# Splitting the parts of w1 on ScalarE and VectorE, a plain F32 transform in the filter, and a first GEMM that ends tile by tile

## The chip, the core and the metric

The kernel runs on one core of one Trainium2 chip. The engines of a core work side by side, each through its own instructions in order: TensorE (PE, matrix products; PEld are its weight loads), VectorE (DVE), ScalarE (ACT), GpSimd (POOL) and SyncE (SP, which here only issues transfers). Transfers (DMA) are issued by SP or by POOL. The metric is the device time of one execution in microseconds; of several runs the median counts. The profile is of one execution and gives its span, from the first to the last instruction. TensorE's granted clock is given as a share of its full clock.

## The reference

Two branches read the same normalised input of 2048 tokens and 512 channels; the output is their product added to the input.

```python
def _A_ref(x, w_r, w_i):
    X = jnp.fft.rfft2(x, axes=(-2, -1))
    X = X * (w_r + 1j * w_i)
    return jnp.fft.irfft2(X, s=(S, D), axes=(-2, -1))

def _B_ref(x, w1, b1, w2, b2):
    h = _layernorm(x, axis=-1)
    u = _gelu(jnp.einsum("bsd,sf->bdf", h, w1) + b1)
    y = jnp.einsum("bdf,fs->bds", u, w2) + b2
    return y.transpose(0, 2, 1)

xn = _layernorm(x, axis=-1)
return x + _A_ref(xn, A_w_r, A_w_i) * _silu(_B_ref(xn, B_w1, B_b1, B_w2, B_b2))
```

S is 2048, D is 512 and the hidden size F is 1792. All of it is float32.

## The kernel before

The tokens lie as 16 blocks `j` of 128 partitions with 512 channels each, the hidden size is cut into 14 tiles of 128. The products of the two GEMMs are made in F32R, a reduced form of float32: each operand is split into a high part (a ScalarE copy into F32R) and a low part (the rest), and `mm3` (L116 to L119) adds three products, high x high, high x low and low x high. The helper `split` (L113) makes both parts, the high one on ScalarE and the low one on VectorE.

There are three stages.

1. **First half of the first GEMM** (loop of L349). For each block `j` the layer norm, the split of the normalised block into `hh[j]` and `hl[j]`, the split of w1's tiles 0 to 3 and 7 to 9, their products into seven of the eight PSUM banks (L316), and the first step of the Fourier transform along the sequence (`first_transform`, L191), folded by VectorE and GpSimd into `ey`.
2. **The filter, and the rest of the first GEMM beside it** (L403 to L562). `filter_steps` (L420) works off 16 groups of frequencies: a transform along the channels (L430, from `ey` and the constant `cd`), its result `sh`/`sl`, the transform along the sequence with the constant `gf` (`mm3`, L439), the multiplication with the filter on VectorE (L450 to L467, with ScalarE copies `zi` and `pq`), and the way back along the sequence (L490). Beside it `hidden_rest` (L523) makes the other seven tiles of the first GEMM in two batches: in the first all blocks `j` for tiles 4, 5, 10 and 11 (banks 7, 2, 0, 1), in the second all `j` for tiles 6, 12 and 13 (banks 7, 0, 1). One block of one batch is a *part*; 32 parts are loaded and split by `w1_part` (L497), three ahead of their use. Tiles 0 to 3 and 7 to 9 go through gelu (L248) at the start of this stage, tiles 4, 5, 10 and 11 between the batches, the rest behind the stage.
3. **The second GEMM** (loop of L693). It goes by a scheme of seven products in place of eight over blocks of 2 x 2: `forms` (L260) makes from the gelu results the tiles `fd`, `fa`, `fb`, `fc` (high and low, sums and differences), `w2_forms` (L593) makes the seven combinations of w2's quarters `a12`, `s1`, `a11`, `s4`, `a21`, each again high and low (L585, L586). One product is 21 instructions of 128x256 (L710), seven tiles times three. The way back of the spectral branch along the channels (L645, constant `ci`) and along the tokens (`spectral`, L668), the silu and the final product with the store run beside it.

`w1_part` is the piece that the change is about most. A raw part comes by SP into one of three buffers `w1s`; ScalarE writes the high part, writes its negative into the place of the low part, and GpSimd issues a transfer that adds the raw part to it:

```python
            A.activation(wq[:, 0], w, AF.Copy)
            A.activation(wq[:, 1], wq[:, 0].bitcast(F32), AF.Copy, scale=-1.0)
            G.dma_start(wq[:, 1], w, accum_op=ALU.add)
```

The order of the work in stage 2 is made by the loop of L549: in 19 steps the filter's generators are moved on with lags of 0, 1 and 3, 48 slots in all, and after each slot `rest` is moved on until 100 of the 112 tile products have been spread evenly over the slots; the last 12 (`LATE`) come behind, block by block (L622). The tile framework's scheduler then orders each engine's instructions. Buffers come from pools: a tile of a new pool in the place of an old one waits until the old tiles there are done with. The pools `us` (gelu results) and `w1q` (parts) take the place of `w1`, which closes at L404; `cd` is loaded at L411, behind that point.

Of the kernel before, what the change touches and what calls it, by code (L numbers as in the profile page):

```python
# [12 lines left out]
ALU = mybir.AluOpType  # L13
# [10 lines left out]
WARM = 16  # L24
LATE = 12
# [17 lines left out]
def _constants():  # L43
# [30 lines left out]
    for lo in range(16):  # L74
# [25 lines left out]
        "c_g": _parts(g, 2),  # L100
# [5 lines left out]
def spectral_mixer_kernel(tc, x, w1, b1, w2, b2, wk, we, wx, c_f, c_ft, c_d, c_i, c_g, c_h, out):  # L106
# [14 lines left out]
    with tc.tile_pool(name="ps", bufs=1, space=PSUM) as psp, ExitStack() as left, ExitStack() as right:  # L121
# [3 lines left out]
        cft = pers.tile([P, 2, P], F32R, name="cft")  # L125
        b1t = pers.tile([P, NF], F32, name="b1t")
# [14 lines left out]
        w1p = pool(lstage, "left", "w1", 3)  # L141
# [74 lines left out]
        def w1_load(j, f0, nf, up, wide):  # L216
            raw = up.tile([P, wide * P], F32, name=f"w1r{f0}_{j}", tag="w1r")
            SY.dma_start(raw[:, :nf * P], w1[:, j, f0 * P:(f0 + nf) * P])
            return raw[:, :nf * P]
# [4 lines left out]
        def hidden(j, banks, w):  # L224
            for i, bank in enumerate(banks):
                sl = slice(i * P, (i + 1) * P)
                mm3(ps[:, bank], w[0][:, sl], w[1][:, sl], hh[j], hl[j], j == 0, j == NJ - 1)
                yield
# [120 lines left out]
        for j in range(NJ):  # L349
# [54 lines left out]
        lstage.close()  # L404
# [3 lines left out]
        usp = pool(lstage, "left", "us", 3)  # L408
        w1q = pool(lstage, "left", "w1q", 3)
        cd = mp.tile([P, 4, P], F32, name="cd", bufs=1)  # L410
        SY.dma_start(cd, c_d)  # L411
# [8 lines left out]
        def filter_steps(n, lo):  # L420
            gf = mp.tile([P, 2, P], F32R, name=f"gf{lo}", tag="gf", bufs=3)
            G.dma_start(gf, c_g[lo])
# [8 lines left out]
            sh = mp.tile([P, D], F32R, name=f"sh{lo}", tag="sh")  # L431
            sl = mp.tile([P, D], F32R, name=f"sl{lo}", tag="sl")
            split(sh, sl, pd)
# [5 lines left out]
            mm3(px, gf[:, 0], gf[:, 1], sh, sl, True, True)  # L439
# [57 lines left out]
        def w1_part(j, runs):  # L497

            n = sum(r[1] for r in runs) * P
            w = w1q.tile([P, 4 * P], F32, name=f"w1s{runs[0][0]}_{j}", tag="w1s")[:, :n]  # L500
            f = 0
            for f0, nf in runs:
                SY.dma_start(w[:, f:f + nf * P], w1[:, j, f0 * P:(f0 + nf) * P])
                f += nf * P
            wq = w1q.tile([P, 2, 4 * P], F32R, name=f"w1q{runs[0][0]}_{j}", tag="w1q", bufs=4)[:, :, :n]
            A.activation(wq[:, 0], w, AF.Copy)  # L506
            A.activation(wq[:, 1], wq[:, 0].bitcast(F32), AF.Copy, scale=-1.0)  # L507
            G.dma_start(wq[:, 1], w, accum_op=ALU.add)  # L508
            return wq[:, 0], wq[:, 1]
# [13 lines left out]
        def hidden_rest():  # L523
            parts_ = [(j, *b) for b in BATCHES for j in range(NJ)]
            w = [w1_part(p[0], p[1]) for p in parts_[:3]]
            for i, (j, runs, banks) in enumerate(parts_):
                yield from hidden(j, banks, w.pop(0))
                if i + 3 < len(parts_):
                    w.append(w1_part(*parts_[i + 3][:2]))
                if i >= NJ:  # L530
                    passed[0] = j + 1
                if i == NJ - 1:
                    while waiting:
                        form_step()
                    for ft, bank in ((10, 0), (11, 1), (4, 7)):
                        gelu(ft, bank)
                    todo.extend([forms(3), forms(4)])
                    waiting.append([(5, 2)])

# [3 lines left out]
        total, done, slot, nslots = 16 * 7 - LATE, 0, 0, 16 * 3  # L543
# [5 lines left out]
        for step in range(16 + 3):  # L549
            if step + 1 < 16:  # L550
                next(chain[step + 1])
            for lag in (0, 1, 3):
                n = step - lag
                if 0 <= n < 16:
                    next(chain[n])
                    slot += 1
                    if slot % 2:
                        form_step()
                    while done * nslots < slot * total:
                        next(rest)  # L560
                        done += 1
# [5 lines left out]
        ORDER = (1, 5, 2, 6, 3, 7, 4)  # L567
# [14 lines left out]
        def w2_form(name, src):  # L582
# [7 lines left out]
               "s4": w2_load("s4", w2p, 0, 1, (NP, 1)), "a21": w2_load("a21", w2p, NP, 0)}  # L590
        cur = dict(nxt)

        def w2_forms():  # L593

            for p in range(NP):
                yield w2_form(f"1_{p}", cur["a12"])
                yield w2_form(f"5_{p}", cur["s1"])
                yield w2_form(f"2_{p}", cur["a11"])
# [16 lines left out]
                if p + 1 < NP:  # L615
                    nxt["a21"] = w2_load("a21", w2p, p + 1 + NP, 0)
# [6 lines left out]
        while todo:  # L623
            form_step()
        for ft, bank in ((12, 0), (13, 1), (6, 7)):
            gelu(ft, bank)
# [4 lines left out]
        ci = fp.tile([P, 4, P], F32, name="ci")  # L631
# [61 lines left out]
        for p in range(NP):  # L693
# [3 lines left out]
            for k, n in enumerate(ORDER):  # L697
# [4 lines left out]
                if k == 2:  # L702
                    yt = gathered(j1)
# [68 lines left out]
```

## Time and profile before

| what | us |
|---|---|
| median of 3 runs | 429.55 |
| lowest and highest run | 425.76, 434.26 |
| the profiled execution | 427.74 |
| its span | 426.0 |
| TensorE busy in it | 394.9 |
| mean granted clock in it | 0.968 of full |

A line of the page's parts and views names the source line of the kernel, the engine, the operation, and what it writes `<-` what it reads. An idle time in square brackets stands ahead of the instruction that ended it, with the engine or transfer that it waited for. A product's busy time is modelled from its start to its last result, so products that follow each other overlap in it: what one of them costs is read from the distance of starts. In a view by stretches of time, the stretch is given in us from the start of the span.

### The profile page before, as it was taken

Reading aid. Unit: us, or ns where it says so; the run is one execution under the profiler, and the core shown is the slowest. Engines: PE = TensorE matmul, PEld = TensorE weight load, DVE = VectorE, ACT = ScalarE, POOL = GpSimd, SP = SyncE. Lnnn points to the kernel's source line nnn. Section 1 sums busy time; section 2 is a strip of 40 time slices with the busy share of each in tenths; the row PEclk is TensorE's granted clock in tenths of the full one; section 3 lists DMA queues with packets and bytes.
Section 4 is the critical chain, followed back from the end, with each engine's and each line's share of the span. In section 5 each row is a group of like instructions: output and inputs, shape, how many; then the busy total and the mean of one; then the engine's idle time right before and its main releaser. Section 6 shows DMA issues by size and latency. Waiting matters only on the chain.

```text
span 426.0 us, 7281 instructions
## 1 busy us (share of the span) xinstructions
PE 394.9 (93%) x2472; PEld 348.3 (82%) x2472; DVE 335.9 (79%) x827; ACT 270.1 (63%) x492; POOL 95.9 (23%) x145
## 2 busy tenths in 40 slices
PE   6899999999498999999996878999999999999995
PEld 3678888888276888788874668999999999999994
DVE  5999999997348878977878257988796969696963
ACT  2556677765856788779886465855565655565631
POOL 3451111111513232323321300202020203120200
PEclk9799999999978999999999996999999999999998
DMA  8644465601968798998877934898796969695612
GB/s 263 212 138 154 144 189 166 195 18 40 261 146 172 189 250 202 239 208 207 198 175 164 284 76 149 226 196 217 178 199 165 204 157 199 184 200 112 116 22 49
DMA packets 39689, 73.11 MB, mean 172 GB/s; under 512 B 4706, under 2 KB 21986, under 8 KB 39524
## 3 DMA queue, kind: packets, MB, share of 16 engines
q1 hardware_dynamic: 28132, 51.81, 39.7%
q0 software_dynamic: 11520, 20.85, 28.7%
q8 instruction: 19, 0.31, 0.3%
q14 instruction: 18, 0.15, 0.1%
HBM read 61.10 MB, written 8.13 MB: 163 GB/s over the span
## 4 chain that ended last, share of the span: by engine, by line
PE 45%; ACT 7%; DMA 6%; DVE 4%; issue 4%; SPq 0%; ACTq 0%; DVEq 0%; POOL 0%; POOLq 0%
PE ps L710 31%; DMA w1s<-in_w_dram 4%; PE ps L645 3%; PE ps L118 3%; PE ps L117 3%; PE ps L119 3%; DMA w1q<-w1s 2%; ACT zi L442 1%; ACT u L248 1%; ACT w1q L507 1%; PE ps L430 1%; ACT w1q L506 1%; ACT zi L441 1%; PE ps L490 1%; DVE w2f L586 1%
## 5 line engine op out<-in xcount | busy, mean ns | idle before, releaser
L316 PE MATMUL ps<-h,w1h 128*128 128x512 f32 x224 | 60.8, 409 | 2.5 <-DVE h L183 1.2
L316 PEld LDWEIGHTS ps<-h,w1h 128*128 128x128 f32 x224 | 41.1, 193 | 13.2 <-ACT h L306 3.4
L119 PE MATMUL ps<-h,w1q 128*128 128x512 f32 x112 | 45.1, 406 | 4.0 <-DMA w1q<-w1s 4.0
L117 PE MATMUL ps<-h,w1q 128*128 128x512 f32 x112 | 47.6, 425 | 0.6 <-ACT u L248 0.4
L710 PE MATMUL ps<-fc,w2f 128*128 128x256 f32 x336 | 44.9, 282 | 2.9 <-ACT fc L253 1.5
L586 DVE TENSOR_TENSOR w2f<-s,w2f 128x896 fp32r<-128x896 f32 x32 | 34.8, 1088 | 16.0 <-ACT w2f L585 16.0
L710 PEld LDWEIGHTS ps<-fc,w2f 128*128 128x128 f32 x336 | 42.6, 190 | 4.8 <-ACT fc L253 1.7
L710 PE MATMUL ps<-fa,w2f 128*128 128x256 f32 x336 | 44.7, 287 | 0.8 <-DVE w2f L586 0.8
L118 PE MATMUL ps<-h,w1q 128*128 128x512 f32 x112 | 44.7, 399 | 0.0
L710 PEld LDWEIGHTS ps<-fa,w2f 128*128 128x128 f32 x336 | 42.1, 193 | 1.2 <-DVE w2f L586 1.1
L710 PE MATMUL ps<-fb,w2f 128*128 128x256 f32 x336 | 42.4, 280 | 0.1
L508 POOL DMA_DIRECT2D w1q<-w1s x32 | 27.7, 875 | 59.9 <-ACT w1q L507 40.9
L710 PEld LDWEIGHTS ps<-fb,w2f 128*128 128x128 f32 x336 | 40.4, 188 | 0.5 <-DVE c L680 0.5
L585 ACT ACTIVATE w2f<-s 128x896 fp32r<-128x896 f32 x32 | 30.3, 949 | 13.9 <-issue 3.9
L586 DVE TENSOR_TENSOR w2f<-a,w2f 128x896 fp32r<-128x896 f32 x24 | 26.1, 1086 | 15.5 <-ACT w2f L585 15.4
L576 POOL DMA_DIRECT2D s<-in_w_dram x16 | 14.3, 893 | 97.8 <-DMA s<-in_w_dram 31.9
L316 PE MATMUL ps<-h,w1l 128*128 128x512 f32 x112 | 31.6, 399 | 0.0
L119 PEld LDWEIGHTS ps<-h,w1q 128*128 128x128 f32 x112 | 21.8, 195 | 9.6 <-DMA w1q<-w1s 4.9
L585 ACT ACTIVATE w2f<-a 128x896 fp32r<-128x896 f32 x24 | 22.7, 948 | 8.2 <-issue 8.2
L506 ACT ACTIVATE w1q<-w1s 128x512 fp32r<-128x512 f32 (+1 forms) x32 | 18.3, 577 | 13.1 <-DMA w1s<-in_w_dram 9.9
L316 PEld LDWEIGHTS ps<-h,w1l 128*128 128x128 f32 x112 | 21.6, 193 | 4.8
L117 PEld LDWEIGHTS ps<-h,w1q 128*128 128x128 f32 x112 | 21.7, 194 | 4.6 <-ACT u L248 0.8
(151 smaller groups left out, 868.0 us busy)
## 6 DMA issues: line engine op xcount, KB each, us to landing
a<-in_w_dram SPq DMA_DIRECT2D x24, 448.0 KB, 4.1
wt<-in_wk_dram SPq DMA_DIRECT2D x16, 512.0 KB, 5.3
s<-in_w_dram SPq DMA_DIRECT2D x16, 448.0 KB, 3.9
s<-in_w_dram POOLq DMA_DIRECT2D x16, 448.0 KB, 6.5
w1s<-in_w_dram SPq DMA_DIRECT2D x48, 128.0 KB, 3.1
w1r<-in_w_dram SPq DMA_DIRECT2D x16, 256.0 KB, 3.1
w1q<-w1s POOLq DMA_DIRECT2D x16, 256.0 KB, 5.2
x<-in_x_dram SPq DMA_DIRECT2D x15, 256.0 KB, 2.8
```

Of the source, the lines that this page charges most:

```text
L117: T.matmul(o, lh, rh, start=first, stop=False)
L118: T.matmul(o, lh, rl, start=False, stop=False)
L119: T.matmul(o, ll, rh, start=False, stop=last)
L248: A.activation(raw[i][:, half], ps[:, bank], AF.Gelu_apprx_tanh, bias=b1t[:, ft:ft + 1])
L316: T.matmul(ps[:, bank + i], w[wi][:, i * P:(i + 1) * P], hj, start=first and j == 0, stop=last and j == NJ - 1)
L506: A.activation(wq[:, 0], w, AF.Copy)
L508: G.dma_start(wq[:, 1], w, accum_op=ALU.add)
L576: G.dma_start(t, w2_half(*added), accum_op=ALU.add)
L585: A.activation(wf[:, 0], v, AF.Copy)
L586: V.tensor_sub(wf[:, 1], v, wf[:, 0].bitcast(F32))
L645: T.matmul(pe[:, b % 2, b // 2], yt[:, b], ci[:, b], start=True, stop=True)
L710: T.matmul(o, wf[:, wi, i], ui, start=m + a == 0 and n in (1, 2, 5), stop=m == NH - 1 and a == 2, skip_group_check=n in (6, 3, 7, 4))
```

## The change

- `w1_part` splits a part as the first half does: ScalarE writes the high part, VectorE subtracts it from the raw part. The second ScalarE pass and the accumulating transfer are gone. (The old way stays in the code behind a flag that is never false.)
- The parts use the tiles `w1r`, `w1h` and `w1l` of the pool `w1` of the first half, which has four buffers in place of three and stays open; `us` lies ahead of it from the start.
- `cd` is loaded at block 4 of the first half. The constant `ci` of the way back is loaded into the same tile later.
- The filter's transform along the sequence is one product in float32 (its constant `gf` whole, issued by SP) in place of three in F32R; `sl` is gone.
- The tile products are paced by weights: the four slots of the last filter steps count twice (`TAIL`). The last 12 go tile by tile, four blocks each, and each tile goes through gelu as soon as it is complete.
- The forms of the second GEMM go 1, 2, 5, 6, 3, 7, 4 in place of 1, 5, 2, 6, 3, 7, 4; the first `a21` is loaded into another pool; `yt` of the second row is gathered one form earlier.

```diff
-        "c_g": _parts(g, 2),
+        "c_g": g.astype(np.float32),
...
-        w1p = pool(lstage, "left", "w1", 3)
+        usp = pool(lstage, "left", "us", 3)
+        w1p = pool(lstage, "left", "w1", 4)
...
+            if j == 4:
+                SY.dma_start(cd, c_d)
...
-            gf = mp.tile([P, 2, P], F32R, name=f"gf{lo}", tag="gf", bufs=3)
-            G.dma_start(gf, c_g[lo])
+            gf = mp.tile([P, P], F32, name=f"gf{lo}", tag="gf", bufs=3)
+            SY.dma_start(gf, c_g[lo])
...
-            split(sh, sl, pd)
+            A.activation(sh, pd, AF.Copy)
...
-            mm3(px, gf[:, 0], gf[:, 1], sh, sl, True, True)
+            T.matmul(px, gf, sh, start=True, stop=True)
...
-            w = w1q.tile([P, 4 * P], F32, name=f"w1s{runs[0][0]}_{j}", tag="w1s")[:, :n]
+            w = w1p.tile([P, 4 * P], F32, name=f"w1s{runs[0][0]}_{j}", tag="w1r", bufs=3)[:, :n]
...
-            wq = w1q.tile([P, 2, 4 * P], F32R, name=f"w1q{runs[0][0]}_{j}", tag="w1q", bufs=4)[:, :, :n]
-            A.activation(wq[:, 0], w, AF.Copy)
-            A.activation(wq[:, 1], wq[:, 0].bitcast(F32), AF.Copy, scale=-1.0)
-            G.dma_start(wq[:, 1], w, accum_op=ALU.add)
-            return wq[:, 0], wq[:, 1]
+            wh, wl = (w1p.tile([P, 4 * P], F32R, name=f"w1{c}{runs[0][0]}_{j}", tag="w1" + c)[:, :n] for c in "hl")
+            if direct:
+                split(wh, wl, w)
...
+            w.append(w1_part(*parts_[-1][:2], True))
+
+            for ft, k, bank in ((12, 1, 0), (13, 2, 1), (6, 0, 7)):
+                for n in range(LATE // 3):
+                    hidden(NJ - LATE // 3 + n, k, bank, w[n])
+                    yield
+                if k == 0:
+                    passed[0] = NJ
+                    while todo:
+                        form_step()
+                gelu(ft, bank)
...
+        weight = {s_: TAIL if s_[0] > 15 else 1 for s_ in steps}
+        whole_weight = sum(weight.values())
...
+            paced += weight[step, lag]
+            while done * whole_weight < paced * total:
+                next(rest)
+                done += 1
...
-        ORDER = (1, 5, 2, 6, 3, 7, 4)
+        ORDER = (1, 2, 5, 6, 3, 7, 4)
...
-        ci = fp.tile([P, 4, P], F32, name="ci")
+        cur["a21"] = w2_load("a21", fp, NP, 0)
+        ci = cd
```

Three places in the order of the instructions. In these rows a tile's name carries the block `j` and a running number; the numbers differ between the two programs. TensorE at the end of the first half, before: the last products of the first half (L316), the filter's first transform (L430), and the first part, whose low half has its own product (L119) only behind three pairs of the others.

```order
L316 MATMUL ps<-h_98,w1h_15_1302 128x512 x3
L430 MATMUL ps<-cd,ey 128x128 x4
L117 MATMUL ps<-h_83,w1q_0_1423 128x512
L118 MATMUL ps<-h_83,w1q_0_1423 128x512
L117 MATMUL ps<-h_83,w1q_0_1423 128x512
L118 MATMUL ps<-h_83,w1q_0_1423 128x512
L117 MATMUL ps<-h_83,w1q_0_1423 128x512
L118 MATMUL ps<-h_83,w1q_0_1423 128x512
L430 MATMUL ps<-cd,ey 128x128
L119 MATMUL ps<-h_83,w1q_0_1423 128x512 x3
```

The same place now; L118 to L120 are `mm3`, L428 is the filter's first transform.

```order
L317 MATMUL ps<-h_102,w1h_15_1307 128x512 x3
L118 MATMUL ps<-h_87,w1h_0_1417 128x512
L119 MATMUL ps<-h_87,w1h_0_1417 128x512
L120 MATMUL ps<-h_87,w1l_0_1418 128x512
L118 MATMUL ps<-h_87,w1h_0_1417 128x512
L119 MATMUL ps<-h_87,w1h_0_1417 128x512
L120 MATMUL ps<-h_87,w1l_0_1418 128x512
L428 MATMUL ps<-cd,ey 128x128 x4
```

Two whole tiles of part 0, low half included, now stand ahead of the filter's first transform.

VectorE in one filter step of the middle of stage 2, before: the filter's multiplication (`xc`, `pq`, `r`), a form's sum (`u`), and the low part `sl`.

```order
L453 SCALAR_TENSOR_TENSOR xc_1844<-zi_1841,ps 128x256
L465 TENSOR_TENSOR s_0_1855<-ps,e_69 128x2
L455 TENSOR_TENSOR xc_1844<-xc_1844,wt_1739 128x1024
L274 TENSOR_TENSOR u_1402<-u_1402 128x256
L456 TENSOR_TENSOR xc_1844<-xc_1844 128x512
L114 TENSOR_TENSOR sl_1914<-ps,sh_1913 128x512
L460 TENSOR_TENSOR pq_1851<-xc_1844 128x4x64
L461 TENSOR_TENSOR r_1852<-xc_1844 128x256
```

The same step now.

```order
L450 SCALAR_TENSOR_TENSOR xc_1805<-zi_1802,ps 128x256
L462 TENSOR_TENSOR s_0_1816<-ps,e_70 128x2
L452 TENSOR_TENSOR xc_1805<-xc_1805,wt_1714 128x1024
L115 TENSOR_TENSOR w1l_10_1860<-w1s_10_1856,w1h_10_1859 128x512
L453 TENSOR_TENSOR xc_1805<-xc_1805 128x512
L115 TENSOR_TENSOR w1l_11_1913<-w1s_11_1909,w1h_11_1912 128x512
L457 TENSOR_TENSOR pq_1812<-xc_1805 128x4x64
L458 TENSOR_TENSOR r_1813<-xc_1805 128x256
```

The low parts of two w1 parts stand inside the chain from `xc` to `pq`, where one `sl` stood.

ScalarE at the end of the first GEMM, before: the last `w1q`, the way back's last copy `ey`, the weight splits (L585), and the three gelus (L248) with the forms of `u_2458` (tiles 5 and 12) and `u_2779` (tiles 6 and 13).

```order
L507 ACTIVATE w1q_15_2741<-w1q_15_2741 128x384
L491 ACTIVATE ey<-ps 128x512
L585 ACTIVATE w2f_0_2716<-a_0_2704 128x896
L248 ACTIVATE u_2779<-ps,b1t 128x512
L248 ACTIVATE u_2458<-ps,b1t 128x512
L253 ACTIVATE fd_2637<-u_2458 128x256
L248 ACTIVATE u_2779<-ps,b1t 128x512
L253 ACTIVATE fd_2784<-u_2779 128x256
L585 ACTIVATE w2f_0_2719<-s_8_2706 128x896
L253 ACTIVATE fa_2787<-u_2458 128x2x256
L253 ACTIVATE fa_2794<-u_2779 128x2x256
```

The same place now; `u_2411` holds tiles 5 and 12, `u_2684` tiles 6 and 13.

```order
L115 ACTIVATE w1h_15_2655<-w1s_15_2652 128x384
L602 ACTIVATE w2f_0_2639<-a_0_2629 128x896
L249 ACTIVATE u_2411<-ps,b1t 128x512
L254 ACTIVATE fd_2582<-u_2411 128x256
L602 ACTIVATE w2f_0_2642<-a_0_2634 128x896
L249 ACTIVATE u_2684<-ps,b1t 128x512
L602 ACTIVATE w2f_0_2778<-s_8_2631 128x896
L254 ACTIVATE fd_2714<-u_2684 128x256
L254 ACTIVATE fa_2717<-u_2411 128x2x256
L249 ACTIVATE u_2684<-ps,b1t 128x512
L254 ACTIVATE fa_2724<-u_2684 128x2x256
```

The three gelus stand apart with forms and weight splits between them; the split of `s_8` (`s1`, which an accumulating transfer completes) stands ahead of the last `fd`.

More of the change, by code (lines that the diff above doesn't have):

```diff
@@ L24 @@
 WARM = 16
+TAIL = 2
 LATE = 12
@@ L125, in spectral_mixer_kernel @@
         cft = pers.tile([P, 2, P], F32R, name="cft")
+        cd = pers.tile([P, 4, P], F32, name="cd")
         b1t = pers.tile([P, NF], F32, name="b1t")
@@ L216, in w1_load @@
         def w1_load(j, f0, nf, up, wide):
-            raw = up.tile([P, wide * P], F32, name=f"w1r{f0}_{j}", tag="w1r")
+            raw = up.tile([P, wide * P], F32, name=f"w1r{f0}_{j}", tag="w1r", bufs=3)
             SY.dma_start(raw[:, :nf * P], w1[:, j, f0 * P:(f0 + nf) * P])
@@ L548, in spectral_mixer_kernel @@
         waiting = [[(3, 3)]]
-        for step in range(16 + 3):
-            if step + 1 < 16:
+        for step, lag in steps:
+            if lag == 0 and step + 1 < 16:
                 next(chain[step + 1])
[L552 to L561, printed above, removed]
+            next(chain[step - lag])
+            slot += 1
+            if slot % 2:
+                form_step()
+            paced += weight[step, lag]
+            while done * whole_weight < paced * total:
+                next(rest)
+                done += 1
         rstage.close()
```

49 lines of the change are left out of this document (24 added, 25 removed).

## The prediction

> **What bounds the kernel now.** I read the page first, then the busy times by stretch, then TensorE's idle times row by row, then the waits of SP.
>
> ```profile
> span 426.0 us, 7281 instructions
> PE 394.9 (93%) x2472; PEld 348.3 (82%) x2472; DVE 335.9 (79%) x827; ACT 270.1 (63%) x492; POOL 95.9 (23%) x145
> ```
>
> TensorE (PE) is the bound, and only its gaps can be won. Columns of the next view: stretch, length, busy time (instructions) of PE, its weight loads, DVE, ACT, POOL, then the granted clock, the DMA share and GB/s.
>
> ```profile
> 40.00:100.00 60.00, 60.00 (x305) 49.53 (x305) 58.48 (x201) 42.20 (x84) 10.64 (x21) 1.00 0.44 141
> 107.00:250.00 143.00, 126.69 (x663) 106.06 (x662) 101.22 (x249) 105.88 (x201) 42.91 (x70) 0.96 0.86 205
> 108.00:124.00 16.00, 9.19 (x36) 7.29 (x37) 5.56 (x11) 10.28 (x21) 4.83 (x9) 0.79 0.85 221
> 132.00:140.00 8.00, 5.98 (x24) 4.79 (x23) 7.00 (x19) 4.69 (x9) 1.61 (x3) 0.79 0.84 197
> 136.00:140.00 4.00, 4.00 (x16) 3.39 (x15) 3.00 (x11) 2.60 (x5) 1.61 (x3) 0.57 0.73 155
> 140.00:222.00 82.00, 80.41 (x445) 68.89 (x444) 67.94 (x169) 66.22 (x127) 25.21 (x41) 1.00 0.87 210
> 222.00:242.00 20.00, 14.46 (x75) 11.25 (x74) 13.41 (x35) 13.71 (x27) 5.71 (x8) 1.00 0.84 210
> 248.00:264.00 16.00, 12.31 (x73) 11.02 (x73) 11.80 (x22) 9.80 (x18) 0.52 (x1) 0.79 0.31 101
> 264.00:420.00 156.00, 155.91 (x1275) 152.10 (x1274) 126.91 (x251) 90.06 (x151) 24.56 (x29) 1.00 0.73 163
> ```
>
> Count as lost the idle time plus (1 - clock) x busy time. The first half of the first GEMM (40 to 100) and the second GEMM (264 to 420) lose nothing to speak of. Between them: 108 to 124 loses 6.8 + 1.9 = **8.7 us**; 132 to 140 loses 2.0 + 1.3 = **3.3**; 140 to 222 **1.6**; 222 to 242 **5.5**; 248 to 264 3.7 + 2.6 = **6.3**. In all 25.4 us, all in the filter stage and at its two ends. What ended the larger gaps:
>
> ```profile
> 110.24 1.13 PE L430 MATMUL ps<-cd,ey 128*128 128x128 f32 x8 [2.58 <-DMA cd<-in_c_d_dram]
> 114.85 0.49 PE L430 MATMUL ps<-cd,ey 128*128 128x128 f32 x2 [1.63 <-DVE sl L114]
> 118.08 1.65 PE L119 MATMUL ps<-h,w1q 128*128 128x512 f32 x3 [2.74 <-DMA w1q<-w1s]
> 135.28 0.49 PE L490 MATMUL ps<-hf,pq 128*128 128x128 f32 x2 [2.02 <-ACT pq L469]
> 232.98 1.16 PE L490 MATMUL ps<-hf,pq 128*128 128x128 f32 x8 [2.41 <-ACT pq L469]
> 241.68 0.50 PE L119 MATMUL ps<-h,w1q 128*128 128x512 f32 x1 [1.23 <-DMA w1q<-w1s]
> 254.85 0.38 PE L710 MATMUL ps<-fc,w2f 128*128 128x256 f32 x1 [1.51 <-ACT fc L253]
> 258.60 3.14 PE L710 MATMUL ps<-fa,w2f 128*128 128x256 f32 x13 [0.81 <-DVE w2f L586]
> ```
>
> Nearly every kind has its cause in the diff: the late load of `cd`, the low part `sl`, the accumulating transfers into `w1q`, and forms that are made only after the last product.
>
> **The w1 parts.** The old path of a part is a load, two ScalarE passes, a POOL issue and an accumulating transfer, and the raw buffer (three of them) comes free only at its end.
>
> ```profile
> L506 ACT ACTIVATE w1q<-w1s 128x512 fp32r<-128x512 f32 (+1 forms) x32 | 18.3, 577 | 13.1 <-DMA w1s<-in_w_dram 9.9
> L507 ACT ACTIVATE w1q<-w1q 128x512 fp32r<-128x512 f32 (+1 forms) x32 | 18.3, 577 | 0.6
> L508 POOL DMA_DIRECT2D w1q<-w1s x32 | 27.7, 875 | 59.9 <-ACT w1q L507 40.9
> w1s<-in_w_dram SPq DMA_DIRECT2D x48, 128.0 KB, 3.1
> w1q<-w1s POOLq DMA_DIRECT2D x16, 256.0 KB, 5.2
> SPq L503 <- DMA w1q<-w1s: 74.4, 24, 7.8
> L309 DVE TENSOR_TENSOR w1l<-w1r,w1h 128x512 fp32r<-128x512 f32 x12 | 8.2, 682 | 0.0
> L309 DVE TENSOR_TENSOR w1l<-w1r,w1h 128x384 fp32r<-128x384 f32 x12 | 8.5, 709 | 0.4
> L114 DVE TENSOR_TENSOR sl<-ps,sh 128x512 fp32r<-128x512 f32 x16 | 11.0, 686 | 8.9 <-ACT sh L114 8.8
> ```
>
> Old turn of a buffer: 3.1 + 0.58 + 0.58 + 0.88 + 5.2 = 10.3 us, over three buffers 3.4 us a part at best; TensorE uses a part in about 143 / 32 = 4.5 us, so any delay shows, and SP's queue stood 74.4 us behind the transfers, with the filter's loads in line behind it. New turn: 3.1 + 0.58 + about 0.7 on DVE = 4.4 us, 1.5 us a part. Removed: 18.3 us of ACT, 27.7 of POOL, 32 transfers. Added: 16 x 0.682 + 16 x 0.709 = 22.3 us of DVE; taken off by the dropped `sl`: 11.0. DVE goes from 101.2 to 112.5 us in this stage, ACT from 105.9 to 87.6. The new DVE work is hidden behind TensorE as long as a part is split before TensorE asks for it; without that cover each part costs its 0.7 us.
>
> **The transform in plain F32.** It replaces three F32R products by one F32 product.
>
> ```profile
> 127.62 0.40 PE L117 MATMUL ps<-sh,gf 128*128 128x512 f32 x1
> 128.32 0.40 PE L118 MATMUL ps<-h,w1q 128*128 128x512 f32 x1
> 238.13 1.16 PE L490 MATMUL ps<-hf,pq 128*128 128x128 f32 x8
> 239.04 0.48 PE L117 MATMUL ps<-h,w1q 128*128 128x512 f32 x1
> 239.36 0.40 PE L118 MATMUL ps<-h,w1q 128*128 128x512 f32 x1
> ```
>
> The old three take 0.70 us (127.62 to 128.32). No row has a 512-column F32 product; the nearest is L490, 512 columns in F32 in eight pieces, 0.91 us, and the F32R product behind it takes 0.32 in place of 0.23. Lower end 0.12 us more each (fewer pieces, 0.82), upper end 0.30 (0.91 + 0.09): 16 x 0.12 to 0.30 = 1.9 to 4.8 us. I take **+3.0**. In return a filter step loses one DVE instruction and its wait. The `gf` loads go from POOL's queue to SP's, halved: 16 issues more on SP, which loses 74 us of standing still.
>
> **The first boundary** (8.7 lost). `cd` comes during the first half, so the 2.58 goes. The first three parts use the old stage's buffers, and their splits stand on ACT and DVE before the end of the first half, in ACT's idle time; the order of TensorE shows products of part 0 with both its halves ahead of the filter. What is late next: the third tile of part 0 needs bank 0, which the last of six gelus frees.
>
> ```profile
> 107.69 3.00 ACT L248 ACTIVATE u<-ps,b1t 128x512 f32<-128x512 f32 x5 [0.27 <-PE ps L316]
> ```
>
> These five began when the first half's last product was done (107.7) and end at 110.7; TensorE is there at 107.7 + 7 x 0.23 + 0.91 = 110.2. I leave 1.0 us: **-7.7**, and the lost clock goes with the gaps.
>
> **The filter.** 132 to 140: the first filter step came late behind the same boundary; I leave 1.0 of 3.3: **-2.3**. 140 to 222 stays at 1.6. 222 to 242: the chain's last steps had too few products beside them and waited for `w1q`. The doubled weight of the last four slots puts more products there; between the last transform and the last second transform now stand 35 products and one group of four, 35 x 0.23 + 0.91 = 9.0 us. I leave 1.5 of 5.5 (the bounds are 0 and 5.5): **-4.0**.
>
> **The second boundary** (6.3 lost).
>
> ```profile
> 247.60 2.70 PE L710 MATMUL ps<-fd,w2f 128*128 128x256 f32 x21
> 250.18 0.51 PE L710 MATMUL ps<-fc,w2f 128*128 128x256 f32 x2
> L248 ACT ACTIVATE u<-ps,b1t 128x512 f32<-128x512 f32 x14 | 9.1, 685 | 6.8 <-PE ps L119 6.5 <-PE ps L316 0.3
> L253 ACT ACTIVATE fa<-u 128x512 fp32r<-128x512 f32 x7 | 4.3, 623 | 0.0
> L585 ACT ACTIVATE w2f<-s 128x896 fp32r<-128x896 f32 x32 | 30.3, 949 | 13.9 <-issue 3.9 <-PE ps L710 3.5 <-ACT g L676 3.4
> SPq L632 <- DVE fb L254: 22.0, 1, 22.0
> ```
>
> A form of the second GEMM takes TensorE 2.6 us (247.60 to 250.18). Finished tile by tile, tiles 12 and 13 go through gelu while the 12 products of the next tile run (2.8 us each). After the last product only gelu 6 (0.69), its `fa` (0.62 + 0.69) and then the weight split and three more high parts (0.95 + 3 x 0.62, + 0.69) follow: the last `fa` is due at six sevenths of the second form, 4.8 us after the last product, and is ready at 2.0; the last `fc` is due at 7.4 and is ready at 4.8, hops between engines apart. The new form order (1, 2, 5) makes that room. `ci`, which waited 22.0 us for space, goes into `cd`'s tile. What can be late: the weight split of `s1` stands on ACT ahead of the last `fd`, and it waits for an accumulating transfer. I leave 1.3: **-5.0**.
>
> **Sum.** 7.7 + 2.3 + 4.0 + 5.0 = 19.0 won, 3.0 paid: 16.0. The profiled execution took 427.74 us (span 426.0), 1.8 under the median of 429.55; 427.74 - 16.0 = 411.7, and I say 412.
>
> **The clock.** After the gap before 135.28 the granted clock from 136 to 140 was 0.57; from 222 to 242, with a gap of 2.41 us, it stayed 1.00. If left gaps of about 2 us at two places cost clock as the first did (1.3 each), 2.6 us are added. The Trainium skill, page "TensorE: Matmul & The Clock Gate", section "Part 1: The HAM clock gate", has the clock halve only after an idle window of about 3.4 us; by it the left gaps, all shorter, would cost no clock and the sum would stay 411.7; by the row of 136 to 140 it would be 414.3. The trace agrees with it at 232.98 and not at 135.28.
>
> **Rivals.** *DVE becomes the bound.* Its long stretch of this stage is 67.94 of 82 us, 0.829. At no more than that, 112.5 us of work need 135.8 of the 143 us: 7.2 won there (the F32 price is hidden in it) and 5.0 behind, **415.5**. For it: the subtractions now stand inside the filter's chain on DVE. Against: from 40 to 100 DVE did 58.48 of 60 us and TensorE lost nothing.
>
> *The parts stay late because of the loads.* ACT waited 9.9 us for plain `w1s` loads, and the DMA share was 0.86. Then only `cd` (2.6) and the second boundary (5.0) are won and 3.0 paid: **423.1**, no change that can be told. Against: the accumulations leave the same DMA engines.
>
> *Slower.* DVE works in order, and a subtraction that waits for a late part holds the filter's chain behind it. The seven waits for `w1s` were 1.4 us each on average (9.9 / 7, where ACT took them); 29 parts x 1.4 = 41 us, **453**. It decides the other way from (16.0 + 8.6) / 29 = 0.85 us a part. Against: three raw buffers now turn round in 4.4 us.
>
> **Chances.** Forecast 0.62, DVE bound 0.22, late loads 0.10, slower 0.05, something else without effect 0.01. 2% of the median is 8.6 us, about what a measurement can tell from no change: under 421.0 is faster, over 438.1 slower. So faster 0.84, same 0.11, slower 0.05. The range goes from 404 (all 25.4 won but for the 1.6, F32 at 1.9: 405.8, less 0.4% of scatter) to 422 (DVE bound, 415.5, with the clock's 2.6 and 1% of scatter).
>
> **What would show it.** Right: TensorE from the first boundary on without gaps over 1 us, the clock at 1.00 from 108 on, the stage some 13 us shorter, no wait of SP for parts, an F32 product at 0.82 to 0.91. Wrong: gaps that end with the low part of w1 or with `pq`, a DVE share over 0.9 with TensorE waiting, ACT standing at the split of `s1`, or a w1 load as the releaser.

## The result, and the profile after

| | before | changed |
|---|---|---|
| median of 4 runs, us | 428.89 | 402.89 |
| lowest and highest, us | 425.76, 434.26 | 400.81, 403.32 |
| profiled execution and its span, us | 427.74, 426.0 | 402.71, 400.9 |

The ratio is 0.9407, 95% interval 0.9341 to 0.9473: faster by 5.9%. The ratios here and below leave out executions that lie more than 1.5% above the fastest of the same kernel. The direction was right; the gain was some 25 us where 16 were forecast, and the time lies 1.1 us below the range.

Busy times on the page of the changed kernel:

```profile
span 400.9 us, 7160 instructions
PE 389.2 (97%) x2456; PEld 341.0 (85%) x2456; DVE 343.5 (86%) x843; ACT 254.4 (63%) x460; POOL 60.0 (15%) x97
```

The span fell by 25.1 us, TensorE's busy time by only 5.7: what went is idle time and half clock. By stretches (columns as in the prediction) the gaps at both ends of the filter stage are gone, and the clock stands at 1.00:

```profile
108.00:124.00 16.00, 16.00 (x85) 12.64 (x84) 12.82 (x31) 13.65 (x27) 1.49 (x5) 1.00 0.54 162
140.00:222.00 82.00, 81.59 (x424) 65.99 (x423) 74.61 (x188) 57.14 (x108) 2.40 (x11) 1.00 0.52 153
107.00:228.00 121.00, 120.59 (x627) 97.73 (x626) 106.12 (x262) 87.29 (x164) 7.35 (x23) 1.00 0.55 157
107.00:230.78 123.78, 123.38 (x647) 100.22 (x645) 107.32 (x264) 89.48 (x168) 7.35 (x23) 1.00 0.55 157
```

TensorE's waits over 0.1 us from 100 us on, in total, times and longest, are three kinds, 1.6 us together:

```profile
PE ps L724 <- DVE fc L255: 1.1, 2, 0.9
PE ps L724 <- DVE fd L255: 0.3, 1, 0.3
PE ps L436 <- DVE s L462: 0.2, 1, 0.2
```

TensorE row by row, at the first boundary, at a transform in plain F32, and at the start of the second GEMM:

```profile
106.94 0.85 PE L317 MATMUL ps<-h,w1h 128*128 128x512 f32 x3
107.63 0.39 PE L118 MATMUL ps<-h,w1h 128*128 128x512 f32 x1
...
109.00 1.05 PE L428 MATMUL ps<-cd,ey 128*128 128x128 f32 x8
109.81 0.70 PE L118 MATMUL ps<-h,w1h 128*128 128x512 f32 x2
...
112.87 1.02 PE L436 MATMUL ps<-sh,gf 128*128 128x512 f32 x2
113.33 0.79 PE L118 MATMUL ps<-h,w1h 128*128 128x512 f32 x1
113.96 0.40 PE L119 MATMUL ps<-h,w1h 128*128 128x512 f32 x1
...
228.16 0.39 PE L120 MATMUL ps<-h,w1l 128*128 128x512 f32 x1
228.38 2.40 PE L724 MATMUL ps<-fd,w2f 128*128 128x256 f32 x19
```

The first product of part 0 starts as the first half's last one hands over (107.63). The F32 product (two rows in the trace) with the product behind it takes 113.96 - 112.87 = 1.09 us; less 0.23 for that product it costs 0.86, 0.16 more than the old three. The second GEMM starts at 228.38 in place of 247.60: 19.2 us of the 25.1 were won by then, 5.9 behind it.

### The profile page after: what moved, and what is told of

The parts are those of the page before. It is cut to its first block, busy times and chain, and to the rows that moved or that the text cites. A ratio compares the mean times of both kernels' runs of the same rounds, so it can differ in the third digit from the quotient of the medians.

```text
span 400.9 us, 7160 instructions
## 1 busy us (share of the span) xinstructions
PE 389.2 (97%) x2456; PEld 341.0 (85%) x2456; DVE 343.5 (86%) x843; ACT 254.4 (63%) x460; POOL 60.0 (15%) x97
## 4 chain that ended last, share of the span: by engine, by line
PE 79%; DVE 11%; DMA 4%; ACT 3%; issue 1%; SPq 1%; DVEq 0%; ACTq 0%; POOLq 0%
PE ps L724 33%; PE ps L317 13%; PE ps L119 6%; PE ps L118 6%; PE ps L120 6%; PE ps L659 4%; PE ps L436 3%; PE ps L428 3%; PE ps L487 3%; DMA s<-in_w_dram 3%; PE ps L194 2%; DVE stm L164 1%; DVE h L310 1%; DMA x<-in_x_dram 1%; DMA w1s<-in_w_dram 1%
## 5 line engine op out<-in xcount | busy, mean ns | idle before, releaser
L317 PE MATMUL ps<-h,w1h 128*128 128x512 f32 x224 | 60.8, 408 | 2.5 <-DVE h L186 1.0
L317 PEld LDWEIGHTS ps<-h,w1h 128*128 128x128 f32 x224 | 41.1, 192 | 13.2 <-ACT h L307 3.5
L118 PE MATMUL ps<-h,w1h 128*128 128x512 f32 x112 | 50.3, 451 | 0.1
L120 PE MATMUL ps<-h,w1l 128*128 128x512 f32 x112 | 45.3, 404 | 0.0
L119 PE MATMUL ps<-h,w1h 128*128 128x512 f32 x112 | 44.3, 395 | 0.0
L724 PE MATMUL ps<-fa,w2f 128*128 128x256 f32 x336 | 43.3, 282 | 0.0
L724 PE MATMUL ps<-fc,w2f 128*128 128x256 f32 x336 | 41.9, 281 | 1.1 <-DVE fc L255 1.1
L724 PEld LDWEIGHTS ps<-fc,w2f 128*128 128x128 f32 x336 | 40.4, 188 | 1.7 <-DVE fc L255 1.5
L317 PE MATMUL ps<-h,w1l 128*128 128x512 f32 x112 | 31.6, 399 | 0.0
L593 POOL DMA_DIRECT2D s<-in_w_dram x16 | 13.8, 861 | 113.7 <-DVE es L664 34.3
L118 PEld LDWEIGHTS ps<-h,w1h 128*128 128x128 f32 x112 | 21.2, 189 | 6.2 <-issue 2.6
L119 PEld LDWEIGHTS ps<-h,w1h 128*128 128x128 f32 x112 | 21.2, 189 | 5.6 <-issue 2.6
L317 PEld LDWEIGHTS ps<-h,w1l 128*128 128x128 f32 x112 | 21.6, 193 | 4.9
L120 PEld LDWEIGHTS ps<-h,w1l 128*128 128x128 f32 x112 | 21.0, 188 | 5.4 <-issue 1.0
L724 PE MATMUL ps<-fd,w2f 128*128 128x256 f32 x168 | 22.2, 281 | 0.3 <-DVE fd L255 0.3
```

The costliest lines, as they stand in the source:

```text
L118: T.matmul(o, lh, rh, start=first, stop=False)
L119: T.matmul(o, lh, rl, start=False, stop=False)
L120: T.matmul(o, ll, rh, start=False, stop=last)
L317: T.matmul(ps[:, bank + i], w[wi][:, i * P:(i + 1) * P], hj, start=first and j == 0, stop=last and j == NJ - 1)
L593: G.dma_start(t, w2_half(*added), accum_op=ALU.add)
L724: T.matmul(o, wf[:, wi, i], ui, start=m + a == 0 and n in (1, 2, 5), stop=m == NH - 1 and a == 2, skip_group_check=n in (6, 3, 7, 4))
```

## The experiments

Medians in us; each ratio is against the kernel before in runs on the same chip. The runs were spread over six chips; how much of a difference between two medians comes from the chip is not shown. The runs of one of these kernels lie within one to four us, those of the kernel before between 423 and 437, so a difference between two rows is read from the medians, and from the traces where it is small. The control is the changed kernel again. The edits are shown shortened.

| run | the edit | median | ratio, 95% interval |
|---|---|---|---|
| e10 | control | 401.5 | 0.939, 0.932 to 0.945 |
| e1 | parts on the old path | 415.1 | 0.974, 0.965 to 0.983 |
| e9 | before + direct split | 409.4 | 0.967, 0.959 to 0.974 |
| e13 | before + direct split + F32 | 411.0 | 0.961, 0.955 to 0.967 |
| e3 | cd's load later in the program | 401.8 | 0.943, 0.936 to 0.950 |
| e2 | end block by block | 402.6 | 0.946, 0.939 to 0.954 |
| e7 | old order of forms | 403.4 | 0.946, 0.942 to 0.950 |
| e8 | weight 1 | 402.1 | 0.943, 0.940 to 0.947 |
| e12 | e2, e7 and e8 together | 405.8 | 0.949, 0.943 to 0.955 |
| e4 | F32 transform twice | 414.4 | 0.973, 0.964 to 0.982 |
| e5 | three F32R products | 410.0 | 0.962, 0.958 to 0.966 |
| e14 | e5 with weight 1 | 406.4 | 0.955, 0.952 to 0.958 |
| e11 | e5, half of the parts' subtractions on POOL | 410.3 | 0.959, 0.953 to 0.965 |
| e6 | 16 unread subtractions that wait for `sh` | 409.5 | 0.961, 0.957 to 0.965 |
| e15 | 16 unread ones that never wait | 408.7 | 0.961, 0.957 to 0.965 |
| e17 | 8 unread ones that never wait | 400.8 | 0.939, 0.932 to 0.945 |

> The changed kernel itself, on the chip of the next three: 401 to 404 us. It fixes the level that differences of one or two us are read against.

The tile framework's scheduler orders each engine anew for every kernel. What a run shows is its edit with that order; differences of one us between medians are not read as an effect.

### Which part carries the gain

**The parts' path, taken back (e1, e16)** and **made alone in the kernel before (e9)**:

```diff
-                split(wh, wl, w)
+                A.activation(wh, w, AF.Copy)
+                A.activation(wl, wh.bitcast(F32), AF.Copy, scale=-1.0)
+                G.dma_start(wl, w, accum_op=ALU.add)
```

> The changed kernel, with the 32 parts of w1 on their old path (ACT copy, ACT negative, accumulating transfer on POOL's queue); everything else of the change stays. Theory A, the parts' path carries most of the gain of the filter stage (changed kernel 402.9 us, before 428.9): SP waits again for accumulations, TensorE waits at the first parts and at the end of the stage, 412 to 418 us, and the granted clock dips again. Theory B, the early cd, the common pool and the tile-by-tile end carry it, and the transfers were hidden all along: 403 to 406 us, since three loads ahead leave three parts of cover.

> The changed kernel with the parts on their old path, once more for its trace (its timed runs gave 415.1 us). Theory A, TensorE waits for the accumulating transfers in the steady state and SP stands behind them: more than 6 us of TensorE's idle time end with them. Theory B, the loss is clock and filter waits, and transfers end little of it: under 3 us.

> The kernel before, with the direct split of the parts alone (their own pool behind the boundary, cd late, low part of s, old end). DVE has 22.3 us more in the stage: 101.2 + 22.3 = 123.5 of 143 us. Theory A, the parts' path alone wins what the gaps with transfers as releasers cost: the stage falls from 140 to some 131 us, 418 to 422 us. Theory B, without the dropped low part of s DVE is too full and the gain is lost: 426 to 430 us. Theory C, the path is nearly all of the gain ahead of the second boundary: 410 to 414 us.

Without it 13.6 us are lost (415.1 against 401.5). It alone in the kernel before makes 409.4, just below the range of theory C: 14 us less by the ratio. Left to all the other edits together are 7.9 us by the medians (409.4 to 401.5), 12 by the ratios (0.967 to 0.939). By the traces, the stage from the first filter product to the second GEMM takes 137.4 us in the kernel before (110.24 to 247.60), 120.9 in e9 (108.99 to 229.85) and 119.2 in the control. One of SP's waits in e16 (e1's kernel once more for its trace, one execution of 412.5 us; total, times, longest), and rows of TensorE:

```profile
SPq L500 <- DMA w1l<-w1s: 59.4, 24, 4.8
```

```profile
208.62 1.13 PE L436 MATMUL ps<-sh,gf 128*128 128x512 f32 x2 [2.35 <-ACT ey L488]
209.15 1.02 PE L118 MATMUL ps<-h,w1h 128*128 128x512 f32 x1
209.97 0.63 PE L119 MATMUL ps<-h,w1h 128*128 128x512 f32 x1
210.40 0.63 PE L120 MATMUL ps<-h,w1l 128*128 128x512 f32 x1
...
231.06 0.79 PE L120 MATMUL ps<-h,w1l 128*128 128x512 f32 x1 [4.52 <-DMA w1l<-w1s]
231.65 0.63 PE L118 MATMUL ps<-h,w1h 128*128 128x512 f32 x1
232.08 0.63 PE L119 MATMUL ps<-h,w1h 128*128 128x512 f32 x1
```

SP stands behind the accumulations again, and of TensorE's idle time 4.52 us end with one, between the two theories' 6 and 3. Behind each of the two gaps the products start 0.43 us apart in place of 0.23: here half clock comes with a gap and is paid on top of it.

**The F32 transform beside the direct split alone (e13)**, in the kernel before:

```diff
-            A.activation(wq[:, 0], w, AF.Copy)
-            A.activation(wq[:, 1], wq[:, 0].bitcast(F32), AF.Copy, scale=-1.0)
-            G.dma_start(wq[:, 1], w, accum_op=ALU.add)
+            split(wq[:, 0], wq[:, 1], w)
...
-            split(sh, sl, pd)
+            A.activation(sh, pd, AF.Copy)
...
-            mm3(px, gf[:, 0], gf[:, 1], sh, sl, True, True)
+            T.matmul(px, gf, sh, start=True, stop=True)
```

> The kernel before, with the direct split of the parts and the plain F32 transform, and nothing else of the change (pool, late cd, end, order and pace as before). The direct split alone gave 409.4 us. Theory A, TensorE bounds, and the F32 product only adds its 2.6 us: 410 to 412.5 us. Theory B, DVE bounds with the direct split alone, and dropping its 11.0 us of low parts wins more than the F32 product costs: 404 to 407.5 us; what is then left to the changed kernel is the worth of the other edits together.

The medians are 411.0 against 409.4, the ratios 0.961 against 0.967, from two chips, and the intervals overlap: the totals do not tell the two apart, and 411.0 is far from theory B's 404 to 407.5. By the traces, one execution each, the stage from the first filter product to the second GEMM takes 232.53 - 109.83 = 122.7 us in e13 and 229.85 - 108.99 = 120.9 in e9: there, with the rest as before, the F32 product costs 1.8 of its 2.6 us net. At the first boundary e13 shows what both keep from the kernel before: the late `cd` holds TensorE for 2.87 us (2.26 in e9), and the products behind it run at half pace.

```profile
106.10 0.85 PE L316 MATMUL ps<-h,w1h 128*128 128x512 f32 x3
109.83 1.65 PE L430 MATMUL ps<-cd,ey 128*128 128x128 f32 x8 [2.87 <-DMA cd<-in_c_d_dram]
111.12 0.77 PE L117 MATMUL ps<-h,w1q 128*128 128x512 f32 x1
111.70 0.63 PE L118 MATMUL ps<-h,w1q 128*128 128x512 f32 x1
112.12 0.63 PE L119 MATMUL ps<-h,w1q 128*128 128x512 f32 x1
```

**cd's load (e3)**, moved in the program from block 4 to behind the first half:

```diff
-            if j == 4:
-                SY.dma_start(cd, c_d)
...
+        SY.dma_start(cd, c_d)
```

> The changed kernel, with cd loaded behind the first half as before. Theory A, only the wait of 2.6 us for cd comes back, with no clock lost, because the first parts are ready and the products of part 0 stand ahead of the filter: 403 to 405.5 us. Theory B, a late cd delays the whole chain and takes clock with it: 407 to 411 us.

401.8: nothing, and the first filter product starts 5.25 us behind the last `cf` product in e3 (102.89 to 108.14) as in the control (102.78 to 108.03). The trace says why. The issue of the load, in e3 and in the kernel before (the times are its start):

```profile
L408 SPq DMA_DIRECT2D cd<-in_c_d_dram x1: 425/425/425, 84.2 to 84.2; - x1
```

```profile
L411 SPq DMA_DIRECT2D cd<-in_c_d_dram x1: 327/327/327, 106.7 to 106.7; - x1
```

`cd` now has a tile of its own, and SP issues its load at 84.2 us, still during the first half and 23.9 us ahead of the first filter product (at 16.4 us in the changed kernel). So the edit did not make `cd` late, and e3 tests neither theory: what a late `cd` would cost the changed kernel is not shown.

**The second boundary (e2, e7, e8, e12)**: old end, old order of the forms, old weight, and all three.

```diff
-                if i == len(parts_) - LATE // 3:
-                    break
...
+        for ft, bank in ((12, 0), (13, 1), (6, 7)):
+            gelu(ft, bank)
...
-TAIL = 2
+TAIL = 1
...
-        ORDER = (1, 2, 5, 6, 3, 7, 4)
+        ORDER = (1, 5, 2, 6, 3, 7, 4)
```

> The changed kernel, with the last twelve products block by block and the three gelus and the last forms behind all of them, as before. Theory A, the second boundary is worth what the distance of starts says: the 5.9 us won behind the last product come back nearly whole, 407.5 to 409.5 us. Theory B, the end was paid for by the form order and the tile of ci more than by the tile-by-tile end: 404 to 406 us.

> The changed kernel, with the old order of the seven forms of the second GEMM (1, 5, 2, 6, 3, 7, 4). Theory A, the new order makes the room for the last forms at the second boundary: without it TensorE waits for the split of s1 behind the first form, 404 to 406 us. Theory B, the tile-by-tile end alone hides it: 402.5 to 403.5 us.

> The changed kernel, with weight 1 for the last four slots of the filter, as before, so that fewer products of the first GEMM stand beside its last steps. Theory A, the gap before the last second transform comes back in part: 404 to 406 us. Theory B, the parts come in time now, and that gap was theirs: 402.5 to 403.5 us.

> The changed kernel with the whole second boundary as before: last twelve products block by block, gelus behind them, old order of the forms, weight 1 for the last slots. Theory A, the tile-by-tile end and the form order each cover for the other, and without both TensorE waits and loses clock behind the last product: 405 to 409 us. Theory B, neither was worth anything; the second boundary's 5.9 us come from weight loads and space that the common pool and ci in cd's tile make free earlier: 402 to 404 us.

Each alone lies 0.6 to 1.9 us above the control, where the changed kernel's own two medians are 1.4 apart (401.5 and 402.9); all together cost 4.3 (405.8). Whether they add up or cover for each other is not told by that. From the start of the second GEMM to the end, one trace each, the control takes 171.8 us, e2 173.5, e7 175.9 (its traced execution was its slowest, 406.0), e12 177.1, the kernel before 178.4. In e12 the second boundary looks as it did before:

```profile
231.77 1.80 PE L715 MATMUL ps<-fc,w2f 128*128 128x256 f32 x13 [0.62 <-DVE w2f L590]
233.41 0.40 PE L715 MATMUL ps<-fa,w2f 128*128 128x256 f32 x2
235.32 0.38 PE L715 MATMUL ps<-fc,w2f 128*128 128x256 f32 x1 [1.51 <-ACT fc L254]
236.26 0.70 PE L715 MATMUL ps<-fc,w2f 128*128 128x256 f32 x3 [0.56 <-DVE fc L255]
237.47 0.80 PE L715 MATMUL ps<-fc,w2f 128*128 128x256 f32 x2 [0.50 <-DVE fc L255]
```

The same stretch of e12 and of the control:

```profile
234.00:242.00 8.00, 5.62 (x25) 5.15 (x26) 7.56 (x18) 5.73 (x11) 0.00 (x0) 0.67 0.36 118
```

```profile
234.00:242.00 8.00, 6.87 (x53) 6.14 (x52) 7.60 (x17) 7.85 (x15) 0.00 (x0) 1.00 0.50 173
```

The four gaps are 3.2 us, and TensorE's clock falls to 0.67 from 234 to 242, another 0.33 x 5.62 = 1.9 us.

### Which engine bounds the stage

**More TensorE (e4)**, the F32 product issued twice:

```diff
             T.matmul(px, gf, sh, start=True, stop=True)
+            T.matmul(px, gf, sh, start=True, stop=True)
```

> The changed kernel, with the F32 product of the transform issued twice into the same bank (the result is that of one). It adds 16 x 0.86 = 13.8 us of TensorE and nothing to another engine. Theory A, TensorE is the only bound of the stage: 416 to 417.5 us. Theory B, DVE or the chain of the filter bounds it in part and TensorE's added time goes partly into gaps: under 413 us.

414.4, 12.8 more than the control. From the first filter product to the second GEMM e4 takes 242.67 - 109.31 = 133.4 us, the control 227.27 - 108.03 = 119.2: 14.1 more, the 13.8 in full: in the stage theory A holds. What lies behind is 2.1 us shorter (169.7 against 171.8): no wait for forms is left there, which was no part of the theory.

**More VectorE (e5, e6, e14, e15, e17, e11).** In e5 and e14 the transform is made of three F32R products, with the low part by VectorE; in e6, e15 and e17 VectorE has a subtraction more that nobody reads. The edits of e5, of e6, and of e15 (e17: only in odd steps):

```diff
-            A.activation(sh, pd, AF.Copy)
+            split(sh, sl, pd)
...
-            T.matmul(px, gf, sh, start=True, stop=True)
+            mm3(px, gf[:, 0], gf[:, 1], sh, sl, True, True)
```

```diff
+            V.tensor_sub(sl, pd, sh)
```

```diff
+            V.tensor_sub(jk, cd, cd)
```

> The changed kernel, with the filter's forward transform again as three F32R products (constants in two parts by POOL's queue, the low part of s by a DVE subtraction inside the chain). TensorE has 16 x 0.16 = 2.6 us less, DVE 11.0 us more (112.5 to 123.5 of some 129 us). Theory A, TensorE is the only bound: 400 to 401 us, so the plain F32 transform is a loss of 2.6 us by itself. Theory B, DVE at 0.96 of the stage becomes the bound and its low part stands in the chain: 404 to 410 us, so the plain F32 transform is what makes room for the parts' splits.

> The changed kernel, with one subtraction of 128x512 more on DVE in each of the 16 filter steps, which nobody reads: DVE has 11.0 us more, TensorE nothing less, and no product waits for it by itself. Theory A, DVE has slack: 402.5 to 404 us. Theory B, DVE is near its bound at 0.87 and 0.96 shows: 405 to 412 us.

> The changed kernel with three F32R products in the forward transform (410.0 us with the pace as changed) and weight 1 for the last four slots, as before. Its waits for the low parts of w1 stood near 212 and 218 us, where the doubled weight asks for most parts per slot. Theory A, DVE's volume in the stage is what costs, wherever the products stand: 408 to 410.5 us. Theory B, only the bunched parts at the end find DVE behind: 402 to 405 us.

> The changed kernel with one more subtraction of 128x512 in each filter step whose inputs are the constant cd, so that it never waits (nobody reads its result). In e6 the same 11.0 us stood where DVE waits 5.9 us for the copy of s, and cost 7 us. Theory A, volume: 407 to 410 us. Theory B, the waits in order for the copy were half of the price: 403 to 406 us.

> The changed kernel with the subtraction of e15 (constant inputs, never waits, nobody reads it) in every second filter step: 8 x 0.69 = 5.5 us more on DVE. Theory A, DVE's slack lets some 4 to 5 us in for nothing and the rest shows (11.0 us cost 7): 402 to 404 us. Theory B, the price is proportional from the first instruction, because each one moves the scheduler's order and delays the parts: 404.5 to 406 us.

The stretch of 107 to 228 us, quoted above for the changed kernel, in e17:

```profile
107.00:228.00 121.00, 120.46 (x628) 97.81 (x627) 110.57 (x270) 86.94 (x164) 8.02 (x22) 1.00 0.55 157
```

In e15:

```profile
107.00:228.00 121.00, 118.73 (x618) 95.76 (x617) 113.90 (x276) 83.97 (x158) 7.53 (x21) 1.00 0.53 154
```

In e5:

```profile
107.00:228.00 121.00, 114.16 (x615) 96.07 (x614) 112.22 (x275) 82.92 (x158) 14.03 (x35) 0.99 0.54 154
```

VectorE's busy time is the third: 106.12 us in the changed kernel. With 110.57 (0.91, e17) nothing is lost, which is better than both theories; with 113.90 (0.94, e15), or with 112.22 and waits for `sh` (e5), 7 to 8.5 us (e6, which has both the unread work and those waits, 8.0). Only a part of this is VectorE being late. In the traces TensorE waits for low parts of w1 for 4.6 us in e5, 4.0 in e6, 2.4 in e14 and 2.2 in e15, and not at all in the control and in e17. Nor does the share alone decide: in e9, where the other edits are missing, VectorE is as full, and TensorE waits for no part of w1:

```profile
107.00:228.00 121.00, 117.99 (x632) 100.36 (x633) 113.82 (x278) 85.33 (x161) 17.20 (x36) 0.99 0.58 166
```

So in the changed kernel there is slack of a few us, and behind it a price; which of the other edits takes e9's tolerance away was not tried. How a late part comes about is seen in SP's waits for the parts' raw buffers, in the changed kernel:

```profile
SPq L500 <- DVE w1l L115: 6.0, 4, 2.7
```

In e5, and behind it TensorE's rows there:

```profile
SPq L501 <- DVE w1l L115: 22.9, 12, 5.3
```

```profile
212.31 0.98 PE L120 MATMUL ps<-h,w1l 128*128 128x512 f32 x3 [1.62 <-DVE w1l L115]
...
218.57 1.65 PE L120 MATMUL ps<-h,w1l 128*128 128x512 f32 x3 [3.00 <-DVE w1l L115]
```

A late subtraction gives its raw buffer back late, SP holds the next load, and the part comes late. (Such waits need not reach TensorE: e9 has 22.3 us of them.)

Weight 1 (e14) takes 3.6 us of e5's 8.5 away and leaves 4.9, so bunching the parts at the end is part of the price, and neither theory of e14 held whole. e15 lies in the range of its theory A, volume, but its trace shows two losses. VectorE is late once, at 215.70. At 231.37 the loss is of another kind: ScalarE, in order, had a weight split ahead of the last part's copy, and that waited for a transfer:

```profile
215.70 0.98 PE L120 MATMUL ps<-h,w1l 128*128 128x512 f32 x3 [2.22 <-DVE w1l L115]
...
231.37 0.50 PE L118 MATMUL ps<-h,w1h 128*128 128x512 f32 x1 [2.35 <-ACT w1h L115]
```

```profile
229.96 0.95 ACT L604 ACTIVATE w2f<-s 128x896 fp32r<-128x896 f32 x1 [3.86 <-DMA s<-in_w_dram]
230.81 0.51 ACT L115 ACTIVATE w1h<-w1s 128x384 fp32r<-128x384 f32 x1
```

In the control that copy stands ahead of the weight splits (at 219.16 us, the first split at 219.58). Behind the second gap the clock is 0.79 from 228 to 236, another 0.21 x 5.65 = 1.2 us. The three make 5.8 of the 6.2 us by which e15's span exceeds the control's (405.3 and 399.1): 2.2 us end with VectorE, the rest with an order that the scheduler made for this kernel, and with the clock behind it. For e5 and e6 the two are not separated.

**POOL to the rescue (e11)**: as e5, with the subtraction of every second part on POOL:

```diff
-                split(wh, wl, w)
+                split(wh, wl, w, G if j % 2 else V)
```

> The changed kernel with the forward transform as three F32R products again, and the subtractions of every second w1 part on POOL (1.28 us and 1.17 us each in the first half's rows) in place of DVE: TensorE 2.6 us less, DVE 123.5 - 9.9 = 113.6 us, POOL some 20 us more. Theory A, the loss of the F32R version (410.0 us) is the volume of DVE alone: 400 to 401.5 us, below the changed kernel. Theory B, the loss is the place of the low part inside the filter's chain, or POOL's subtractions come too late: 404 to 410 us.

410.3, no better than e5. VectorE's busy time did not fall: 113.40 us from 107 to 228, against 112.22 in e5, with 16 instructions fewer. Some of its instructions grew longer (the mean in ns stands behind the busy time; e5 has 684 and 683 for these two):

```profile
L454 DVE TENSOR_TENSOR xc<-xc 128x512 f32<-128x512 f32 x16 | 12.4, 776 | 0.0
...
L115 DVE TENSOR_TENSOR w1l<-w1s,w1h 128x512 fp32r<-128x512 f32 x6 | 6.7, 1109 | 0.0
```

The Trainium skill, page "GPSIMD Engine Reference", section "1. Specifications", says that POOL's SBUF interfaces are shared with VectorE and contend with its instructions of two SBUF inputs; these rows agree.

## Where the prediction was right, and which steps failed

The mechanism was right: TensorE's gaps were what there was to win, and nearly all went. What failed is the size of the sum: 16.0 us were forecast and the span fell by 25.1, so the time came out below the range. Two steps carry most of the missing 9.1 us, the count of what is lost (4.2) and the allowances for what would stay (3.7); the second boundary (0.9) and the F32 price (0.4) make up the rest. Counting starts of products, not busy times, shows them. From the first half's last hand-over to the second GEMM the kernel before takes 247.60 - 107.49 = 140.1 us, the changed one 228.38 - 107.63 = 120.75. The work itself, estimated from such distances as 336 products of w1 at 0.2285 us, three transforms a step (0.81 + 0.81 + 0.70, now 0.86) and 0.09 for each of 32 changes from F32 back to F32R, is 116.8 and 119.4. So 23.3 us were lost before, and 1.4 are lost now.

- **"Count as lost the idle time plus (1 - clock) x busy time."** The four stretches of the stage gave 19.1 us (8.7 + 3.3 + 1.6 + 5.5); 23.3 were lost. This step is 4.2 short. One row over the whole stage, before, would have shown half of it (16.31 us idle + 0.04 x 123.80 = 21.3):

```profile
107.49:247.60 140.11, 123.80 (x642) 103.48 (x642) 100.32 (x247) 103.15 (x195) 42.42 (x70) 0.96 0.86 207
```

The rest fits the modelled ends, which is argued and not shown: a product counts 0.39 us where the next starts after 0.23, so the last one ahead of each gap hides 0.16 us of it.

- **The allowances "I leave 1.0", "1.0 of 3.3", 1.6 and 1.5.** They are 5.1 us; 1.4 stayed lost. This is 3.7 more. The 1.0 at the first boundary was for a wait for bank 0 at 110.2: the rows show TensorE on L118 at 109.81 with no wait.
- **The second boundary, -5.0**: 5.9 in the trace (178.4 to 172.5 us from the second GEMM's start). e12 bears the reasoning out: with everything old there 4.3 us come back, as gaps and as clock.
- **The F32 transform, +3.0**: 16 x 0.16 = 2.6, inside the 0.12 to 0.30. That its return is only a DVE instruction and its wait was too little said: without it the changed kernel takes 406.4 to 410.0 us (e14, e5), and TensorE waits 2.4 to 4.6 us for low parts of w1. It costs TensorE 2.6 us and frees 11.0 of VectorE. Beside the direct split alone it showed no such return (e13).
- **"DVE goes from 101.2 to 112.5 us in this stage"**: too high: the stretch that ends as far behind the start of the second GEMM as the prediction's 250 (107 to 230.78) shows 107.32. The splits of 128x384 took 0.553 us there, not the 0.709 of the first half's rows (16 x 0.156 = 2.5 us), and three of the 128x512 ones lie ahead of 107 (2.1). The rival that VectorE is full at 0.829 was wrong as a limit: 0.91 costs nothing (e17). It was near as a danger: a few us more bring waits for low parts of 2.2 to 4.6 us (e5, e6, e14, e15).
- **Slower through VectorE's order**: did not come; a part held up behind a wait in order appears in e15, on ScalarE, and costs 2.35 us there.
- **Loads too late**: no. The `w1s` loads land after 2.6 us in place of 3.1, the DMA share is 0.55 in place of 0.86.
- **"`cd` comes during the first half, so the 2.58 goes."** It does, and the gap went. e3 does not test it, since its load comes during the first half too. In the kernel before with new edits the gap still stands (2.87 us in e13).

The clock: gaps of 0.50 to 1.51 us went with 0.67 in e12, and gaps of 2.35 and 2.87 us with half the pace in e16 and e13. The Trainium skill, page "TensorE: Matmul & The Clock Gate", section "Part 1: The HAM clock gate", asks for an idle window of about 3.4 us; these rows do not agree, the gap of 4.52 us in e16 does. The 2.6 us that the range kept for half clock were needless all the same, because no such gaps were left.

## What to carry over

Count lost time on a bound engine by distances of starts against the sum of its work, over the whole stage; busy shares of picked stretches understate it, and a short gap can cost as much again in clock. Undo small edits together as well as one at a time: singly each may drown in the scatter. Read from the trace whether an edit did what it was meant to do before its time is taken for an answer: e3 did not make the load late, and more than half of e15's loss hangs on ScalarE's order. An edit that slows the bound engine by a little can pay for another that fills its neighbour (e5 and e14 against the control), and elsewhere pay nothing (e13 against e9).

## What had not been expected of the hardware

- A subtraction on POOL lengthened those on VectorE (683 to 1109 ns for a 128x512 split on average), so that moving 16 of them relieved nothing.
- Gaps well under 3 us cost clock at some places (0.67 in 234 to 242 of e12), while in the kernel before the gap of 2.41 us at 232.98 cost none in its stretch (1.00 from 222 to 242). What tells them apart stays open.
